# Sigmoid attention and a squared-ReLU FFN on one core: attn @ v in 64 x 64 quarters of the array, with an accumulator for each pair of heads

## The chip, the core and the metric

The kernel runs on one core of a Trainium2 chip, in one launch. The metric is the device time of that core in microseconds (us). Three executions of the kernel before gave 1017.53, 1017.70 and 1017.81 us; their median is 1017.7.

## What is computed

Eight batches of 12 heads, 448 positions and 64 dimensions a head, then a feed-forward network over 3584 tokens; all of it is float32.

```python
def _attn_ref(q, k, v):
    scale = 1.0 / np.sqrt(q.shape[-1])
    scores = scale * np.matmul(q, k.transpose(0, 1, 3, 2)) - np.log(S)
    attn = 1.0 / (1.0 + np.exp(-scores))
    return np.matmul(attn, v)

def _moe_ref(x, w_in, w_out, s, b):
    r = np.maximum(x @ w_in, 0.0)
    return (s * (r * r) + b) @ w_out
```

There is no softmax: each score goes through a sigmoid by itself, so that a block of keys can be finished alone. The change touches the attention only.

## The kernel before

The work has three stages that follow each other on TensorE: the attention (up to 251 us of the span), the FFN on the first 512 tokens, done plainly (to about 380 us), and the FFN on the other 3072 tokens, whose products are formed from sums of weight and token blocks (to the end). While TensorE does the attention, VectorE (DVE) and ScalarE (ACT) also convert the FFN's weights and form sums of weight rows; which step does how many of these jobs is set by the list `PIECES` and by `sums_out`, and `ticks(n, ...)` puts them into the engines' queues.

The attention takes 24 steps, one for each batch and each four heads ("quad"). Four heads are two pairs; `i` counts the pairs and `j` the two heads of a pair. The 448 keys of a head are three full blocks of 128 (`c` = 0, 1, 2) and a last block of 64. The last blocks of the two pairs share one tile.

One step does this, in this order on TensorE:

- `scores` (L658): keys times queries for six (pair, block) places, in the rounded high and low parts of the float32 numbers, three products each (`PARTS`), two heads at once in the two row halves of the array (64 x 128). Each place is a PSUM tile of two banks, a head in each. ACT makes the sigmoid of each (L638) into a tile `a` in SBUF.
- `attn_v` (L692): for each pair and each block, `v` (128 keys x 64 dimensions) times `a` (128 keys x 448 queries) in plain float32. A matmul fills the array's 128 rows and half of its columns, so the two heads of a pair run at once (128 x 64). A float32 matmul of the program is two matmul instructions in the trace. All of it accumulates in one PSUM tile `pav` of two banks: a bank for each pair, 64 partitions for each head.
- `scores_last` (L679): the scores of the last blocks of the *next* step, in 64 x 64 quarters, all four heads at once; ACT makes the sigmoid `a_l`.
- `attn_v_last` (L701): the last blocks of *this* step, also in quarters, added to `pav`, with the `a_l` that the step before made.

PSUM's eight banks are four tiles of two: three rotate as `psc` (scores and last scores), and the fourth is `pav`, which one score place, pair 0 with block 2, uses before `attn_v` does.

ACT's queue in a step: six sigmoids; the rounding of the next step's q and k (`qkh`, L621); the step's conversions (`wf`, L446) and roundings of weight sums (`t`, L491); the sigmoid `a_l`. DVE's queue: conversions and sums for the step; `parts_lo`, the low parts of the next step's q and k (`qkl`, L421), which needs `qkh`; the copy of `pav` to SBUF (`store_x`, L708), after which SyncE (SP) sends it to DRAM. Every engine takes its instructions in the order written, and a wait stops all that stand behind it in that queue.

Of the kernel before, what the change touches and what calls it, by code (L numbers as in the profile page):

```python
# [11 lines left out]
F32 = mybir.dt.float32  # L12
# [7 lines left out]
PSUM = bass.MemoryType.PSUM  # L20
# [308 lines left out]
def sigmoid_attention_relu2_ffn(  # L329
# [10 lines left out]
    nc = tc.nc  # L340
    B, NQ, P, _, _, S = qk.shape
    D = v.shape[5]
    NF, _, DM = w_in.shape
# [14 lines left out]
    def pool(stack, name, bufs, side=None, space=None):  # L358
        kw = dict(side=side) if side else {}
        if space is not None:  # L360
            kw["space"] = space
        return stack.enter_context(
            tc.tile_pool(name=name, bufs=bufs, reuse_waits="tile", **kw)
        )
# [41 lines left out]
    x_dram = [dram.tile([P, NCC, S], F32, name=f"xd_{b}") for b in range(B)]  # L406
# [10 lines left out]
    def add(o, x, y):  # L417
        nc.vector.tensor_tensor(o, x, y, op=ALU.add)  # L418
# [5 lines left out]
    order = [f + h * NP for f in range(NP) for h in range(2)]  # L424
# [159 lines left out]
    xo = pool(at, "xo", 2)  # L584
    ldv = pool(at, "ldv", 2)
    qkx = ExitStack()
    ld = pool(qkx, "ld", 2)
    hl = pool(qkx, "hl", 1)
    ps_qk = pool(qkx, "ps_qk", 3, space=PSUM)
    ps_av = pool(at, "ps_av", 1, space=PSUM, side="right")  # L590

    half = (slice(0, D), slice(D, P))
    quads = [(b, t) for b in range(B) for t in range(NQ)]
    NL = len(quads)

    def load(b, t, first=False):
        x = ld.tile([P, 2, 2, S], F32, tag="qk", name=f"qk_{b}_{t}")
        if first:
            nc.sync.dma_start(x[:, 0, 1, :P], qk[b, t][:, 0, 1, :P])
            nc.scalar.dma_start(x[:, 0, 0], qk[b, t][:, 0, 0])  # L600
            nc.sync.dma_start(x[:, 0, 1, P:], qk[b, t][:, 0, 1, P:])
            nc.scalar.dma_start(x[:, 1, 0], qk[b, t][:, 1, 0])
            nc.sync.dma_start(x[:, 1, 1], qk[b, t][:, 1, 1])
        else:
            nc.sync.dma_start(x, qk[b, t])
        return [x]

    def load_v(b, t, ld_):
        vt = ldv.tile([P, 7, 2, D], F32, tag="v", name=f"v_{b}_{t}")
        nc.sync.dma_start(vt, v[b, t])  # L610
        ld_.append(vt)
# [6 lines left out]
    def parts_hi(b, t, ld_):  # L618

        hi, lo = (hl.tile([P, 2, NX], F32R, tag=h, name=f"qk{h}_{b}_{t}") for h in "hl")  # L620
        nc.scalar.copy(hi, flat(ld_[0]))  # L621
        ld_.append((hi, lo))

    def parts_lo(ld_):
        hi, lo = ld_[-1]
        sub(lo, flat(ld_[0]), f32(hi))

    def parts_dve(b, t, ld_, pieces):
        hi, lo = (hl.tile([P, 2, NX], F32R, tag=h, name=f"qk{h}_{b}_{t}") for h in "hl")
        x = flat(ld_[0])  # L630
        for i, cols in pieces:
            nc.vector.tensor_copy(hi[:, i, cols], x[:, i, cols])
            sub(lo[:, i, cols], x[:, i, cols], f32(hi[:, i, cols]))
        ld_.append((hi, lo))

    def sigmoid(psc, name):
        a = ap_.tile([P, 2, S], F32, tag="a", name=f"a_{name}")
        nc.scalar.activation(a, psc[:, :, :S], AF.Sigmoid, bias=nls, scale=SCALE)  # L638
        return a

    def scores(b, t, ld_):
        x = ld_[0]
        two = ld_.pop() if len(ld_) > 2 else None
        whole = two is None or (b, t) == quads[0]
        a = {}
        psc = {}
        order = [(i, c) for i in range(2) for c in range(3)]
        if not whole:
            order[2:4] = order[3], order[2]
        for i, c in order:  # L650

            pl, tag = (ps_av, "pav") if (i, c) == (0, 2) else (ps_qk, "psc")
            o = psc[i, c] = pl.tile([P, 2, 512], F32, tag=tag, name=f"psc_{b}_{t}_{i}_{c}")
            if two and (i or c == 2 or not whole):
                cols = slice(S + c * P, S + (c + 1) * P)
                for m, (wi, xi) in enumerate(PARTS):
                    for j, r in enumerate(half):
                        nc.tensor.matmul(  # L658
                            o[:, j, :S], two[wi][r, i, cols], two[xi][r, i, :S],
                            start=m == 0, stop=m == 2,  # L660
                        )
            else:
                for j, r in enumerate(half):
                    nc.tensor.matmul(  # L664
                        o[:, j, :S], x[r, i, 1, c * P : (c + 1) * P], x[r, i, 0, :],
                        start=True, stop=True,
                    )
            if not whole and (i, c) == (1, 0):
                continue
            for k in [(i, c)] + [(1, 0)] * (not whole and (i, c) == (0, 2)):  # L670
                a[k] = sigmoid(psc[k], f"{b}_{t}_{k[0]}_{k[1]}")
        return a

    def scores_last(b, t, ld_):
        x = ld_[0]
        psc = ps_qk.tile([P, 2, 512], F32, tag="psc", name=f"psc_{b}_{t}_l")
        for j, r in enumerate(half):
            for i in range(2):
                nc.tensor.matmul(  # L679
                    psc[half[i], j, :S], x[r, i, 1, 3 * P :], x[r, i, 0, :],  # L680
                    start=True, stop=True,
                )
        return sigmoid(psc, f"{b}_{t}_l")

    def attn_v(b, t, ld_, a, between=None):
        pav = ps_av.tile([P, 2, 512], F32, tag="pav", name=f"pav_{b}_{t}")
        for i in range(2):
            if i and between:
                between()
            for c in range(3):  # L690
                for j, r in enumerate(half):
                    nc.tensor.matmul(  # L692
                        pav[r, i, :S], ld_[1][:, 3 * i + c, j, :], a[i, c][:, j, :],
                        start=c == 0, stop=False,
                    )
        return pav

    def attn_v_last(ld_, a, pav):
        for i in range(2):
            for j, r in enumerate(half):  # L700
                nc.tensor.matmul(  # L701
                    pav[r, i, :S], ld_[1][half[i], 6, j, :], a[half[i], j, :],
                    start=False, stop=True,
                )

    def store_x(b, t, pav):
        o = xo.tile([P, 2, S], F32, tag="xo", name=f"xo_{b}_{t}")
        nc.vector.tensor_copy(o, pav[:, :, :S])  # L708
        nc.sync.dma_start(x_dram[b][:, 2 * t : 2 * t + 2], o)

    loaded = {0: load(*quads[0], first=True)}
    load_v(*quads[0], loaded[0])
# [1 line left out]
    nc.scalar.activation(e_bias, nls, AF.Sigmoid)  # L714
    nc.vector.memset(e_bias, -896.0 * 2.0**23)

    idle = ps_qk.tile([P, 2, 512], F32, tag="psc", name="idle")
    ones = nc.const_aps.tensor(1.0, [P, 512], BF16)
    for _ in range(WARM):
        nc.tensor.matmul(idle[:, 0, :S], ones[:, :P], ones[:, :S], start=True, stop=True)  # L720
# [11 lines left out]
    def ticks(n, part):  # L732
        for _, _, fn in sorted(plan.pop((n, part), ()), key=lambda x: x[:2]):
            fn()
# [114 lines left out]
    for n, (b, t) in enumerate(quads):  # L849
        if n:  # L850
            ticks(n, "DVE")
        a = scores(b, t, loaded[n])
        between = None
        if n == 0:
            parts_dve(*quads[1], loaded[1], [(i, slice(NX)) for i in range(2)])
            ticks(0, "DVE")
            firsts = []

            def between():
                firsts.append(scores_last(*quads[0], loaded[0]))  # L860
                ticks(0, "ACT")

        else:
            if n + 1 in TWO:
                parts_hi(*quads[n + 1], loaded[n + 1])
            ticks(n, "ACT")
        if n + 2 < NL:
            loaded[n + 2] = load(*quads[n + 2])
        ticks(n, "SP")
        for fn in stores:  # L870
            fn()
        stores.clear()
        if n == NL - 1:
            qkx.close()
            ps_h = pool(blk_ps, "ps_h", 2, space=PSUM)
        pav = attn_v(b, t, loaded[n], a, between)
        last = al if n else firsts[0]
        if n + 1 < NL:
            al = scores_last(*quads[n + 1], loaded[n + 1])
        attn_v_last(loaded[n], last, pav)  # L880
        if n and n + 1 in TWO:
            parts_lo(loaded[n + 1])
        ticks(n, "END")
        store_x(b, t, pav)
        if n + 2 < NL:
            load_v(*quads[n + 2], loaded[n + 2])
    ph0 = ffn1(order[0], w1[0])
# [364 lines left out]
    for a, *_ in PRODUCTS_1:  # L1252
        seen = [a]
        while seen:
            x = seen.pop(0)
# [178 lines left out]
    o = plan1.op("SP", 0.0, readers, opened, late=OPEN_DUE)  # L1434
# [3 lines left out]
    x = None  # L1438
    for k in range(AHEAD):
        _, l, row, p = stream[k]  # L1440
        after = [o, x] + [row_op.get((l, row, f)) for f in (2 * p, 2 * p + 1)]
        x = plan1.op("SP", 1.28, after, lambda at: fetch(), late=OPEN_DUE + 6.0 + 2.8 * k)
# [84 lines left out]
```

## Time and profile before

| | before |
|---|---|
| median of three executions | 1017.7 us |
| the profiled execution: its own time | 1018.07 us |
| the profiled execution: its span | 1016.3 us |
| outside the span | 1.8 us |
| TensorE busy in the span | 1012.1 us |
| DVE busy in the span | 879.7 us |
| ACT busy in the span | 717.0 us |
| granted clock of TensorE | 1.00 |

The trace's times are in us from the span's start. A row of the timeline gives the start, the duration, the engine, the line, the operation, the tile written and the tiles read, the shape, and how many instructions in a row were merged; the square bracket behind it is the time for which the engine stood idle before them and whose end released it. Matmuls overlap: a row's duration runs to the end of its last instruction, so the next row starts before it. In the chain of waits each row is the stretch of the path that ended last. A group row gives the count of instructions, their busy time, the mean duration of one in ns, and the idle time before them.

### The profile page before, as it was taken

Reading aid. Unit: us, or ns where it says so; the run is one execution under the profiler, and the core shown is the slowest. Engines: PE = TensorE matmul, PEld = TensorE weight load, DVE = VectorE, ACT = ScalarE, POOL = GpSimd, SP = SyncE. Lnnn points to the kernel's source line nnn. Section 1 sums busy time; section 2 is a strip of 40 time slices with the busy share of each in tenths; the row PEclk is TensorE's granted clock in tenths of the full one; section 3 lists DMA queues with packets and bytes.
Section 4 is the critical chain, followed back from the end, with each engine's and each line's share of the span. In section 5 each row is a group of like instructions: output and inputs, shape, how many; then the busy total and the mean of one; then the engine's idle time right before and its main releaser. Section 6 shows DMA issues by size and latency. Waiting matters only on the chain.

```text
span 1016.3 us, 13837 instructions
## 1 busy us (share of the span) xinstructions
PE 1012.1 (100%) x5194; PEld 762.7 (75%) x5194; DVE 879.7 (87%) x989; ACT 717.0 (71%) x772; POOL 0.2 (0%) x4
## 2 busy tenths in 40 slices
PE   9999999999999999999999999999999999999998
PEld 4545455555888888888888888888888888888887
DVE  5899999898999958999978999996668668899995
ACT  7889999899777757747999944424544979964430
POOL 0000000000000000000000000000000000000000
PEclk9999999999999999999999999999999999999999
DMA  9788999896999999998966666799676666666784
GB/s 338 261 306 303 327 338 390 316 359 245 347 408 348 336 395 382 354 346 280 302 193 201 189 192 200 238 364 309 209 213 198 190 193 198 190 192 199 209 248 164
DMA packets 101073, 278.77 MB, mean 274 GB/s; under 512 B 10000, under 2 KB 23184, under 8 KB 101008
## 3 DMA queue, kind: packets, MB, share of 16 engines
q1 hardware_dynamic: 100720, 277.45, 79.9%
q8 instruction: 41, 0.67, 0.3%
q10 hardware_dynamic: 288, 0.46, 0.1%
q14 instruction: 24, 0.20, 0.1%
HBM read 193.99 MB, written 83.89 MB: 273 GB/s over the span
## 4 chain that ended last, share of the span: by engine, by line
PE 99%; ACT 1%; issue 0%; DVE 0%; ACTq 0%
PE b L1009 31%; PE b L1018 31%; PE pav L692 11%; PE psc L658 9%; PE ph L818 6%; PE po L1271 6%; PE psc_l L679 2%; PE pav L701 2%; ACT a L638 0%; PE idle L720 0%; PE psc L664 0%; PE o L1032 0%; ACT wf L446 0%; ACT qkh L621 0%; ACT t L491 0%
## 5 line engine op out<-in xcount | busy, mean ns | idle before, releaser
L1009 PE MATMUL b<-o_0h,wu 128*128 128x512 f32 x928 | 286.0, 389 | 0.0
L1009 PEld LDWEIGHTS b<-o_0h,wu 128*128 128x128 f32 x928 | 174.2, 188 | 36.2
L1009 PE MATMUL b<-o_0l,wu 128*128 128x512 f32 x464 | 180.5, 389 | 0.0
L1018 PE MATMUL b<-o_0h,wu 128*128 128x512 f32 x464 | 152.3, 389 | 0.0
L1018 PE MATMUL b<-o_1h,wu 128*128 128x512 f32 x456 | 149.6, 389 | 0.0
L638 ACT ACTIVATE a<-psc,nls 128x896 f32<-128x896 f32 x144 | 132.8, 1009 | 13.3 <-PE psc L658 10.6
L692 PE MATMUL pav<-a,v 128*64 128x448 f32 x576 | 113.8, 543 | 0.0
L418 DVE TENSOR_TENSOR r<-r,b 128x1024 f32<-128x1024 f32 x74 | 89.6, 1217 | 25.8 <-PE b L1009 22.9
L1009 PEld LDWEIGHTS b<-o_0l,wu 128*128 128x128 f32 x464 | 87.1, 188 | 18.0
L1018 PEld LDWEIGHTS b<-o_0h,wu 128*128 128x128 f32 x464 | 87.1, 188 | 18.0
L1018 PEld LDWEIGHTS b<-o_1h,wu 128*128 128x128 f32 x456 | 85.7, 188 | 17.7
L421 DVE TENSOR_TENSOR r<-r,b 128x1024 f32<-128x1024 f32 x66 | 80.0, 1216 | 20.4 <-PE b L1018 11.7
L1018 PE MATMUL b<-o_0l,wu 128*128 128x512 f32 x232 | 90.2, 389 | 0.0
L1018 PE MATMUL b<-o_1l,wu 128*128 128x512 f32 x228 | 88.7, 389 | 0.0
L692 PEld LDWEIGHTS pav<-a,v 128*64 128x64 f32 x576 | 39.1, 137 | 63.9 <-issue 45.1
L1064 ACT ACTIVATE r<-b 128x1024 f32<-128x1024 f32 x46 | 46.3, 1026 | 31.9 <-DVE r L418 13.4
L1271 PE MATMUL po<-g,w 128*128 128x512 f32 x288 | 67.7, 389 | 0.0
L959 ACT CAST o_0h<-r 128x1024 fp32r<-128x1024 f32 x26 | 27.3, 1051 | 57.2 <-DVE r L421 35.3
L1271 PEld LDWEIGHTS po<-g,w 128*128 128x128 f32 x288 | 54.1, 188 | 11.2
L491 ACT CAST t<-t 128x768 fp32r<-128x768 f32 (+2 forms) x62 | 44.1, 730 | 25.7 <-DVE t L421 15.7
L818 PE MATMUL ph<-x0h,w 128*128 128x512 f32 x192 | 61.7, 390 | 0.0
L1138 ACT ACTIVATE r<-r,b_sb,s_sb 128x1024 f32<-128x1024 f32 x48 | 59.5, 1241 | 1.0
(115 smaller groups left out, 1693.9 us busy)
## 6 DMA issues: line engine op xcount, KB each, us to landing
wu<-wd SPq DMA_DIRECT2D x232, 512.0 KB, 4.3
wd<-t SPq DMA_DIRECT2D x36, 768.0 KB, 6.8
qk<-qk_t SPq DMA_DIRECT2D x23, 896.0 KB, 7.0
st<-w_out SPq DMA_DIRECT2D x16, 768.0 KB, 8.7
st<-w_in SPq DMA_DIRECT2D x16, 768.0 KB, 9.0
wd<-t SPq DMA_DIRECT2D x22, 512.0 KB, 5.0
v<-v_t SPq DMA_DIRECT2D x24, 448.0 KB, 5.5
xd<-xo SPq DMA_DIRECT2D x24, 448.0 KB, 3.6
```

Source lines behind the costliest of these rows:

```text
L418: nc.vector.tensor_tensor(o, x, y, op=ALU.add)
L421: nc.vector.tensor_tensor(o, x, y, op=ALU.subtract)
L491: nc.scalar.copy(ts[g][:, :n, 0], f32(ts[g][:, :n, 1]))
L638: nc.scalar.activation(a, psc[:, :, :S], AF.Sigmoid, bias=nls, scale=SCALE)
L658: nc.tensor.matmul(o[:, j, :S], two[wi][r, i, cols], two[xi][r, i, :S], start=m == 0, stop=m == 2,)
L692: nc.tensor.matmul(pav[r, i, :S], ld_[1][:, 3 * i + c, j, :], a[i, c][:, j, :], start=c == 0, stop=False,)
L818: nc.tensor.matmul(ph, w[:, k, wi, kc * P : (kc + 1) * P], x0[h][xi][:, cc, :], start=m == 0, stop=m == 3 * NCC - 1,)
L1009: nc.tensor.matmul(bk[:, j], wt[:, j, wi, c * P : (c + 1) * P], tiles[xi][:, c, :], start=first and m == 0, stop=m == 3 * KC - 1, skip_gro ...
L1018: nc.tensor.matmul(bk[:, e], wt[:, f, wi, e * P : (e + 1) * P], tiles[gi][:, f], start=first and f == 0 and m == 0, stop=p == np_ - 1 and ...
L1064: nc.scalar.activation(v.t, bank_t[b], AF.Copy, scale=-1.0)
L1138: nc.scalar.activation(v.t, v.t, AF.Identity, bias=b_sb, scale=s_sb)
L1271: nc.tensor.matmul(pos[e], w[:, k, wi, kc * P : (kc + 1) * P], g[:, gi, :], start=first and i == 0, stop=last and i == 2,)
```

## The change

`attn_v` splits each block of 128 keys into two halves of 64 (`m`, `rows`), so that its matmuls are 64 x 64 quarters, four at once: two key halves times two heads. The two key halves of a pair go to different banks of a PSUM tile that the pair has for itself: `pav` becomes a list of two tiles, and the sum of a pair's two banks is its result. There are twice as many matmuls, each on half as many rows.

For pair `i` the bank `1 - i` is complete when `attn_v` of that pair is done, and is copied out at once into half of an SBUF tile `x`: by DVE for pair 0, in the middle of `attn_v`, and by ACT for pair 1, at its end. `attn_v_last` adds the last block to bank `i`, and then `store_x` has DVE add bank `i` to the half of `x`, once for each pair, in place of one copy of both.

The four two-bank places of PSUM are now named 0 to 3 (`place`); 2 and 3 are those of `pav`. The six score places of a step take the places `turn`, 2, 3 and `turn` again; for every step but the first, pair 1's block 0 stands before pair 0's block 2, and so takes place 3. `scores_last` takes the first of `turn`, which is then reversed.

```diff
-    ps_qk = pool(qkx, "ps_qk", 3, space=PSUM)
+    ps_qk = pool(qkx, "ps_qk", 1, space=PSUM)
     ps_av = pool(at, "ps_av", 1, space=PSUM, side="right")
+    turn = [0, 1]
+    def place(k, name):
+        pl = ps_qk if k < 2 else ps_av
+        return pl.tile([P, 2, 512], F32, tag=f"s{k}", name=name)
...
-        for i, c in order:
-            pl, tag = (ps_av, "pav") if (i, c) == (0, 2) else (ps_qk, "psc")
-            o = psc[i, c] = pl.tile([P, 2, 512], F32, tag=tag, name=f"psc_{b}_{t}_{i}_{c}")
+        places = turn + [2, 3] + turn
+        if not whole:
+            places[2:4] = 3, 2
+        for k, (i, c) in zip(places, order):
+            o = psc[i, c] = place(k, f"psc_{b}_{t}_{i}_{c}")
...
     def attn_v(b, t, ld_, a, between=None):
-        pav = ps_av.tile([P, 2, 512], F32, tag="pav", name=f"pav_{b}_{t}")
+        pav = []
+        x = xo.tile([P, 2, S], F32, tag="xo", name=f"xo_{b}_{t}")
         for i in range(2):
             if i and between:
                 between()
+            o = place(2 + i, f"pav_{b}_{t}_{i}")
+            pav.append(o)
             for c in range(3):
-                for j, r in enumerate(half):
-                    nc.tensor.matmul(
-                        pav[r, i, :S], ld_[1][:, 3 * i + c, j, :], a[i, c][:, j, :],
-                        start=c == 0, stop=False,
-                    )
-        return pav
+                for m, rows in enumerate(half):
+                    for j, r in enumerate(half):
+                        nc.tensor.matmul(
+                            o[r, m, :S], ld_[1][rows, 3 * i + c, j, :], a[i, c][rows, j, :],
+                            start=c == 0, stop=c == 2 and m != i,
+                        )
+            (nc.scalar.copy if i else nc.vector.tensor_copy)(x[:, i], o[:, 1 - i, :S])
+        return pav, x
     def attn_v_last(ld_, a, pav):
         for i in range(2):
             for j, r in enumerate(half):
                 nc.tensor.matmul(
-                    pav[r, i, :S], ld_[1][half[i], 6, j, :], a[half[i], j, :],
+                    pav[i][r, i, :S], ld_[1][half[i], 6, j, :], a[half[i], j, :],
                     start=False, stop=True,
                 )
-    def store_x(b, t, pav):
-        o = xo.tile([P, 2, S], F32, tag="xo", name=f"xo_{b}_{t}")
-        nc.vector.tensor_copy(o, pav[:, :, :S])
-        nc.sync.dma_start(x_dram[b][:, 2 * t : 2 * t + 2], o)
+    def store_x(b, t, pav, x):
+        for i in range(2):
+            add(x[:, i], x[:, i], pav[i][:, i, :S])
+        nc.sync.dma_start(x_dram[b][:, 2 * t : 2 * t + 2], x)
...
-            al = scores_last(*quads[n + 1], loaded[n + 1])
+            al = scores_last(*quads[n + 1], loaded[n + 1], turn[n == 0])
+            if n:
+                turn.reverse()
```

On TensorE, at the end of step 1 before the change (the names give batch, quad, pair and block; `a_1_l` is the sigmoid of the last blocks, `v` the values; a bracket names the engines or transfers whose semaphores the instruction waits for):

```order
L692 MATMUL pav_1_352<-a_1_1_1_333,v_1_173 64x448 [waits Activation_49]
L692 MATMUL pav_1_352<-a_1_1_1_333,v_1_173 64x448
L692 MATMUL pav_1_352<-a_1_1_2_342,v_1_173 64x448 [waits Activation_49]
L692 MATMUL pav_1_352<-a_1_1_2_342,v_1_173 64x448
L679 MATMUL psc_2_l<-qk_2_241 64x448 [waits DMAHW4_49]
L679 MATMUL psc_2_l<-qk_2_241 64x448 x3
L701 MATMUL pav_1_352<-a_1_l,v_1_173 64x448 x4
```

The same place after the change, on TensorE:

```order
L703 MATMUL pav_1_1_383<-a_1_1_1_349,v_1_173 64x448 [waits Activation_49]
L703 MATMUL pav_1_1_383<-a_1_1_1_349,v_1_173 64x448 x3
L703 MATMUL pav_1_1_383<-a_1_1_2_358,v_1_173 64x448 [waits Activation_49]
L703 MATMUL pav_1_1_383<-a_1_1_2_358,v_1_173 64x448 x3
L686 MATMUL psc_2_l<-qk_2_241 64x448 [waits DMAHW4_49,PE_49]
L686 MATMUL psc_2_l<-qk_2_241 64x448 x3
L713 MATMUL pav_1_0_369<-a_1_l,v_1_173 64x448 [waits DVE_49]
L713 MATMUL pav_1_0_369<-a_1_l,v_1_173 64x448
L713 MATMUL pav_1_1_383<-a_1_l,v_1_173 64x448 [waits Activation_49]
L713 MATMUL pav_1_1_383<-a_1_l,v_1_173 64x448
```

Each pair and block has four matmuls where it had two, and the last blocks' four matmuls, which waited for nothing, now wait for DVE (the first two) and for ACT (the other two).

On ACT, in the same step before the change, from the last score sigmoid to the next step's first one:

```order
L638 ACTIVATE a_1_1_2_342<-psc_1_1_2_335,nls 128x896 [waits PE_49,Activation_49]
L621 CAST qkh_2_344<-qk_2_241 128x1664 [waits DMAHW4_49]
L446 ACTIVATE wf_8_99<-wf_8_99,e_bias 128x768 [waits DVE_49]
L638 ACTIVATE a_2_l<-psc_2_l,nls 128x896 [waits PE_49,Activation_49]
L638 ACTIVATE a_2_0_0_396<-psc_2_0_0_389,nls 128x896 [waits PE_49,Activation_49]
```

And after the change, on ACT:

```order
L644 ACTIVATE a_1_1_2_358<-psc_1_1_2_351,nls 128x896 [waits PE_49,Activation_49]
L627 CAST qkh_2_360<-qk_2_241 128x1664 [waits DMAHW4_49]
L446 ACTIVATE wf_8_99<-wf_8_99,e_bias 128x768 [waits DVE_49]
L707 COPY xo_1_368<-pav_1_1_383 128x448 [waits PE_49]
L644 ACTIVATE a_2_l<-psc_2_l,nls 128x896 [waits PE_49,Activation_49]
L644 ACTIVATE a_2_0_0_428<-psc_2_0_0_421,nls 128x896 [waits PE_49,Activation_49]
```

The copy of pair 1's finished bank stands behind the rounding and the conversions of its step, and ahead of `a_l`.

On DVE, around the end of step 1, after the change; before it, two rows stood between the same neighbours, the subtraction `qkl` and one copy of 896 elements a partition (L708):

```order
L442 TENSOR_SCALAR wf_8_99<-st_8_243 128x768 [waits DMAHW5_49]
L707 COPY xo_1_368<-pav_1_0_369 128x448 [waits PE_49]
L421 TENSOR_TENSOR qkl_2_361<-qk_2_241,qkh_2_360 128x1664 [waits DMAHW4_49,Activation_49]
L418 TENSOR_TENSOR xo_1_368<-xo_1_368,pav_1_0_369 128x448 [waits DVE_49,PE_49]
L418 TENSOR_TENSOR xo_1_368<-xo_1_368,pav_1_1_383 128x448 [waits PE_49,Activation_49]
L455 SCALAR_TENSOR_TENSOR st_4_171<-st_4_171 128x768
```

The first copy stands ahead of `qkl`, and the two additions stand where the one copy stood.

More of the change, by code (lines that the diff above doesn't have):

```diff
@@ L672, in scores, with scores_last @@
         return a
-    def scores_last(b, t, ld_):
+    def scores_last(b, t, ld_, k):
         x = ld_[0]
-        psc = ps_qk.tile([P, 2, 512], F32, tag="psc", name=f"psc_{b}_{t}_l")
+        psc = place(k, f"psc_{b}_{t}_l")
         for j, r in enumerate(half):
@@ L715, in sigmoid_attention_relu2_ffn @@
     nc.vector.memset(e_bias, -896.0 * 2.0**23)
-    idle = ps_qk.tile([P, 2, 512], F32, tag="psc", name="idle")
+    idle = place(1, "idle")
     ones = nc.const_aps.tensor(1.0, [P, 512], BF16)
@@ L859, in between @@
             def between():
-                firsts.append(scores_last(*quads[0], loaded[0]))
+                firsts.append(scores_last(*quads[0], loaded[0], 0))
                 ticks(0, "ACT")
@@ L875, in sigmoid_attention_relu2_ffn @@
             ps_h = pool(blk_ps, "ps_h", 2, space=PSUM)
-        pav = attn_v(b, t, loaded[n], a, between)
+        pav, x = attn_v(b, t, loaded[n], a, between)
         last = al if n else firsts[0]
         if n + 1 < NL:
-            al = scores_last(*quads[n + 1], loaded[n + 1])
+            al = scores_last(*quads[n + 1], loaded[n + 1], turn[n == 0])
+            if n:
+                turn.reverse()
         attn_v_last(loaded[n], last, pav)
@@ L883, in sigmoid_attention_relu2_ffn @@
         ticks(n, "END")
-        store_x(b, t, pav)
+        store_x(b, t, pav, x)
         if n + 2 < NL:
```

## The prediction, made before the changed kernel was run

> **What bounds the kernel now.** I read the page first, then the chain of waits, then the timeline of TensorE, ACT and DVE in steps of the attention. The page's busy shares and its chain:
>
> ```profile
> PE 1012.1 (100%) x5194; PEld 762.7 (75%) x5194; DVE 879.7 (87%) x989; ACT 717.0 (71%) x772; POOL 0.2 (0%) x4
> PE 99%; ACT 1%; issue 0%; DVE 0%; ACTq 0%
> ```
>
> TensorE is the whole path: whatever makes it stand still, or lets it work less, shows in the time. The chain of waits in order of time gives the starts of steps 2, 3 and 23 (the six places of the scores, L658), and the last blocks' scores of step 3:
>
> ```profile
> 26.89 3.84 PE psc L658 x36
> ...
> 37.08 3.84 PE psc L658 x36
> ...
> 45.61 0.91 PE psc_l L679 x8
> ...
> 241.88 3.84 PE psc L658 x36
> ```
>
> A step takes 37.08 - 26.89 = 10.19 us where nothing is late. Over 21 steps it is (241.88 - 26.89) / 21 = 10.24, so about 1.0 us of waiting lies in all of them. The timeline of TensorE at the end of step 1; the first row is from a wider window:
>
> ```profile
> 20.50 4.73 PE L692 MATMUL pav<-a,v 128*64 128x448 f32 x24
> ...
> 24.68 0.55 PE L692 MATMUL pav<-a,v 128*64 128x448 f32 x2
> 25.16 0.98 PE L679 MATMUL psc_l<-qk 64*64 64x448 f32 x8
> 25.96 0.93 PE L701 MATMUL pav<-a_l,v 64*64 64x448 f32 x8
> 26.82 0.47 PE L658 MATMUL psc<-qkh 64*128 64x448 f32 x2
> ```
>
> The 24 instructions of `attn_v` run in 12 rounds of two. The last round starts at 24.68, so eleven took 4.18 us, 0.38 each. In quarters four run at once: eight instructions are two rounds, and L679's two took 25.96 - 25.16 = 0.80.
>
> **What the quarters save.** `attn_v` will have 48 instructions, four at a time, which is again 12 rounds of 0.38 us: splitting the keys saves no array time. What goes is the change of shape from 128 x 64 to 64 x 64. The last round of `attn_v` kept the array for 25.16 - 24.68 = 0.48 instead of 0.38, and L679's two rounds took 0.80 instead of 0.76: 0.14 us together. There are 26 such places (one a step, two more in step 0, where the last blocks of step 0 stand inside `attn_v`): **-3.6 us**. The changes between scores and `attn_v`, and back, remain.
>
> **What the early copy costs.** In the changed order the last blocks' matmuls (L713) wait, for pair 1, for ACT's copy of the finished bank. Behind them on TensorE stands the whole next step. The copy can't start before `attn_v` ends, and it stands behind all other ACT work of the step. What covers it is `scores_last`, 0.76 us. ACT at the end of step 0 and of step 1:
>
> ```profile
> 16.02 1.01 ACT L638 ACTIVATE a_l<-psc_l,nls 128x896 f32<-128x896 f32 x1 [0.32 <-PE psc_l L679]
> ...
> 23.00 1.60 ACT L621 CAST qkh<-qk 128x1664 fp32r<-128x1664 f32 x1
> 24.47 0.96 ACT L446 ACTIVATE wf<-wf,e_bias 128x768 int32<-128x768 int32 x1
> 26.27 1.01 ACT L638 ACTIVATE a_l<-psc_l,nls 128x896 f32<-128x896 f32 x1 [0.83 <-PE psc_l L679]
> ```
>
> Copies by ACT out of PSUM, 512 and 1024 columns, in the groups up to 390 us:
>
> ```profile
> L1062 ACT COPY r<-b 128x1024 f32<-128x1024 f32 x2 | 2.0, 1006 | 0.1
> L1484 ACT COPY o<-po 128x512 f32<-128x512 f32 x3 | 1.8, 609 | 0.0
> ```
>
> That is 0.78 ns a column, so 448 columns take 609 - 50 = 0.56 us. Step 1 is a light one: `scores_last` would start at 24.68 + 0.38 = 25.06, and the last blocks would want to start at 25.82. ACT's conversion ends at 25.43; the next instruction starts about 0.1 before such an end (24.47 against 23.00 + 1.60 = 24.60), so the copy runs from 25.36 (its data are there 0.13 after the end of `attn_v`, as `a_l` came 0.13 after 25.16 + 0.98) to 25.92, and TensorE goes on 0.07 later, at 25.99. The stall is **0.17 us**, which is already more than the saved 0.14. Heavier steps, 3 and 9: ACT's last jobs and its `a_l`, and for step 9 TensorE's `scores_last` and where TensorE waited for `a_l`, each from its own timeline:
>
> ```profile
> 44.86 1.78 ACT L446 ACTIVATE wf<-wf,e_bias 128x768 int32<-128x768 int32 x2
> 46.59 1.01 ACT L638 ACTIVATE a_l<-psc_l,nls 128x896 f32<-128x896 f32 x1
> ```
>
> ```profile
> 107.95 1.57 ACT L491 CAST t<-t 128x768 fp32r<-128x768 f32 x2
> 109.41 1.02 ACT L638 ACTIVATE a_l<-psc_l,nls 128x896 f32<-128x896 f32 x1
> ```
>
> ```profile
> 106.96 0.98 PE L679 MATMUL psc_l<-qk 64*64 64x448 f32 x8
> ...
> 110.48 0.47 PE L658 MATMUL psc<-qkh 64*128 64x448 f32 x2 [0.37 <-ACT a_l L638]
> ```
>
> In step 3 ACT is free at about 46.54. Step 3 is two steps behind step 1 (`scores_last` stands at 45.61 in the chain, and for step 1 `attn_v` ends at 24.68 + 0.55 = 25.23), so TensorE wants to go on at 46.20 and can at 46.54 + 0.56 + 0.07 = 47.17: 0.97. In step 9 the places are 107.62 and 110.05: 2.43. Before, such lateness fell on `a_l`, which nobody needs before the next step's third place; 2.4 us of it cost 0.37. Now TensorE stands behind it at once. Each job beyond the light step's one conversion so adds its whole time to the stall. These are ACT's jobs in steps 1 to 22:
>
> ```profile
> L446 ACT ACTIVATE wf<-wf,e_bias 128x768 int32<-128x768 int32 x28 | 25.8, 951 | 0.1
> L638 ACT ACTIVATE a_l<-psc_l,nls 128x896 f32<-128x896 f32 x22 | 22.2, 1009 | 7.4 <-PE psc_l L679 7.3
> L491 ACT CAST t<-t 128x768 fp32r<-128x768 f32 x10 | 8.1, 836 | 0.0
> L832 ACT CAST x0h<-x0l 128x1536 fp32r<-128x1536 f32 x1 | 1.5, 1503 | 0.0
> L547 ACT CAST w<-wf 128x768 fp32r<-128x768 f32 x1 | 0.9, 857 | 0.0
> L491 ACT CAST t<-t 128x256 fp32r<-128x256 f32 x1 | 0.4, 398 | 0.0
> ```
>
> 41 jobs, 36.7 us busy. Less one conversion of 0.95 in each of 22 steps (20.9) and the overlap of 0.11 for each of the 19 others (2.1) that is 13.7 us, and with 22 light stalls of 0.17 (3.7) **+17.4 us**. A stall doesn't heal by itself: every step's sigmoids start after its own first scores, so ACT's lateness is made anew in each step. Step 0 has `a_l` waiting 0.32 instead of 0.83, so 0.51 later: 0.17 + 0.51, say **+0.6**. In step 23 there are no further last scores, so nothing covers the copy; the ACT job ahead of it and TensorE there:
>
> ```profile
> 251.39 0.83 ACT L547 CAST w<-wf 128x768 fp32r<-128x768 f32 x1
> ```
>
> ```profile
> 245.68 4.73 PE L692 MATMUL pav<-a,v 128*64 128x448 f32 x24
> 250.34 0.98 PE L701 MATMUL pav<-a_l,v 64*64 64x448 f32 x8
> ```
>
> TensorE would go on at 250.24, and can at 252.12 + 0.56 + 0.07 = 252.75: **+2.5**. As TensorE now waits ahead of `a_l`, the 1.0 us that it waited before goes: **-1.0**.
>
> **DVE.** Its copy of 896 columns becomes a copy and two additions of 448. The rows nearest, the last two for 1024 and 512 columns:
>
> ```profile
> L708 DVE COPY xo<-pav 128x896 f32<-128x896 f32 x24 | 26.2, 1092 | 11.6 <-PE pav L701 11.6
> ```
>
> ```profile
> L418 DVE TENSOR_TENSOR r<-r,b 128x1024 f32<-128x1024 f32 x74 | 89.6, 1217 | 25.8 <-PE b L1009 22.9
> ```
>
> ```profile
> L421 DVE TENSOR_TENSOR g<-r,g 128x512 fp32r<-128x512 f32 x16 | 11.1, 691 | 15.8 <-ACT g L1343 15.4
> ```
>
> At 1.03 ns a column 448 take 0.63 us, 0.55 from one to the next. The second addition ends 0.07 + 0.55 + 0.63 = 1.25 us after the step's end, where the place of pair 1, block 0 (the third, two times 0.61 us and a change of shape later) is wanted at about 1.25 too; with the hand-over 0.04 a step, **+0.9**. The first copy waits for the middle of `attn_v`, and `qkl` and the rest of DVE's queue stand behind it. Its cover is the time in which DVE waits for ACT's cast. Step 11, one of the tightest:
>
> ```profile
> 126.85 0.56 DVE L442 TENSOR_SCALAR wf<-st 128x768 int32<-128x768 int32 x1
> 127.50 1.89 DVE L421 TENSOR_TENSOR qkl<-qk,qkh 128x1664 fp32r<-128x1664 f32 x1
> 129.83 1.09 DVE L708 COPY xo<-pav 128x896 f32<-128x896 f32 x1 [0.43 <-PE pav L701]
> ```
>
> The copy puts `qkl` off by about 0.5 us, and 0.43 is left behind it: it ends at the step's end, just in time. I take **+1.0** for all steps; the bounds are 0 (the stalls give DVE time) and 0.4 (the half microsecond with little to hide it) in each of nine light steps, by the wait of `a_l` for its scores, which is left only there:
>
> ```profile
> ACT a_l L638 <- PE psc_l L679: 7.3, 10, 0.8
> ```
>
> 7.3 us in steps 1 to 22, 0.8 at most, are some nine light steps.
>
> **The sum.** -3.6 + 17.4 + 0.6 + 2.5 - 1.0 + 0.9 + 1.0 = +17.8 us. The profiled execution's own 1018.07 becomes 1035.9. That one stands 0.4 above the median of the runs, so the median becomes 1017.7 + 17.8 = **1035.5**. Copy time not shown at this size: by the nearest ACT rows it lies between 0.40 (256 columns, the cast above) and 0.61 (512), which over 24 steps is -3.8 to +1.2; I take the slope between two copies out of PSUM.
>
> A page speaks against the wait itself. The Trainium skill, "PSUM — Partial Sum Buffer", Summary, says that PSUM may be read while a matmul runs if the read targets another bank. The early copy reads the bank that the last blocks don't write, so by that page the two could overlap. No trace of before shows such an overlap in one tile. The order after has the wait all the same, so the sum goes by the order.
>
> **Rivals.**
> - *The copy's wait is met early* (0.07): the order names engines, not counts; if ACT's semaphore at L713 stands for `a_l`, made a step before, nothing waits for the copy. Then -3.6 - 1.0 + 0.9 + 1.0 remain: **1015.0**, faster. Against it: pair 0's matmul, which reads the same `a_l`, waits for DVE alone. It decides if all stalls stay under 4 us, which needs ACT idle at the end of `attn_v` in nearly every step; ACT is busy past it in some 13 of 22 steps. The rule above gives the same 1015.0, if this wait were not there.
> - *DVE becomes the bound* (0.08): it gains 0.63 + 1.10 - 1.01 = 0.7 us a step, and the copy parts its work into two waits. If the nine light steps pay 0.6 each rather than the 1.0 in all: 1035.5 + 4.4 = **1039.9**.
> - *TensorE can't issue quarters fast enough* (0.05): the scores run 36 matmuls and 36 weight loads in 3.84 us, 53 ns each; a steady stream of quarters needs 96 in 4.56, 48 ns. At 53, `attn_v` takes 0.5 us longer in each of 24 steps, +12, of which the copy, then less late in the 13 heavy steps, gives back about 6.5: **1041**.
> - *They cancel* (0.02): the stalls only outweigh the saved switches.
>
> **The numbers.** The forecast has 0.78. The range takes in the copy's lower bound with DVE's terms at nothing (1035.5 - 3.8 - 1.9 = 1029.8) and a little more for ACT lateness that shrinks, and above both slower rivals: 1027 to 1043. 0.2% is 2 us, about what a measurement of this kernel can tell. Faster 0.07, same 0.02, slower 0.78 + 0.08 + 0.05 = 0.91.
>
> **What would show it.** TensorE idle before L713 with ACT's xo copy (L707) as releaser, about 0.2 us in light steps and 1 to 2.5 in heavy ones, some 20 us in all; rounds of `attn_v` still 0.38; no gap of 0.1 before L686; a light step of about 10.25. Rounds under 0.36, or no idle time before L713, would make it wrong.

## The result, and the profile after

The changed kernel takes 1033.92 us (median of six runs, 1033.49 to 1035.12); the kernel before, on the same chip, 1017.65 (six runs, 1017.52 to 1017.86). The ratio is 1.0162, with a 95% interval of 1.0149 to 1.0176: slower by 16.3 us. The profiled execution took 1034.05 us, its span is 1032.2, and the granted clock is 1.00 as before.

The page's busy times and the chain's shares by engine:

```profile
PE 1023.0 (99%) x5770; PEld 770.3 (75%) x5770; DVE 894.7 (87%) x1037; ACT 726.7 (70%) x796; POOL 0.2 (0%) x4
PE 91%; ACT 5%; DMA 1%; issue 1%; DVE 1%; SPq 0%; ACTq 0%; DVEq 0%
```

ACT now holds 5% of the path, where it held 1%. The chain of waits in order of time shows where. Steps 2, 3 and 4 start at 27.36, 37.58 and 48.60; then comes step 9, from its first sigmoid to the next step's scores:

```profile
27.36 3.90 PE psc L665 x36
...
37.58 3.87 PE psc L665 x36
...
48.60 3.91 PE psc L665 x36
...
102.82 0.57 ACT a L644
...
109.72 1.78 ACT wf L446 x2
111.50 1.45 ACT t L491 x2
112.95 0.44 ACT xo L707
113.44 0.97 PE pav L713 x4
114.41 3.84 PE psc L665 x36
```

Step 2 is a light one and takes 37.58 - 27.36 = 10.22 us, about as before (10.19). Step 3 has one conversion more on ACT and takes 48.60 - 37.58 = 11.02. In step 9, which has four jobs, the path leaves TensorE from the first sigmoid to the copy and runs through ACT's sigmoids, cast, jobs and copy: the step takes 12.5 us, where before it took 10.2.

The waits of the attention, of the engines that stand for one another (engine, tile and line; releaser; us in total, times, longest):

```profile
ACT a L644 <- PE psc L665: 21.0, 23, 1.3
...
PEld pav L713 <- ACT xo L707: 16.5, 15, 2.2
...
PE pav L713 <- ACT xo L707: 5.0, 7, 1.5
```

The weight loads for the last blocks (PEld) stand 16.5 us behind ACT's copy, in 15 steps. The row of PE shows such waits a second time, on the matmuls: in step 9 the weight loads stand from 111.20 and the matmuls from 111.98, both to 113.44, so the two rows can't be added. And ACT stands for TensorE in each of 23 steps, 21.0 us in all, for the first scores of the next step. Before the change it stood there too, but half as long, and TensorE's matmuls stood for the sigmoid of the last scores in one step only:

```profile
ACT a L638 <- PE psc L658: 10.6, 19, 0.9
...
PE psc L658 <- ACT a_l L638: 0.4, 1, 0.4
```

Now the two wait for one another in step after step.

The quarters did as was said. TensorE at the end of step 1:

```profile
24.04 1.68 PE L703 MATMUL pav<-a,v 64*64 64x448 f32 x16
25.55 0.93 PE L686 MATMUL psc_l<-qk 64*64 64x448 f32 x8
26.30 1.07 PE L713 MATMUL pav<-a_l,v 64*64 64x448 f32 x8
27.29 0.47 PE L665 MATMUL psc<-qkh 64*128 64x448 f32 x2
```

16 instructions are four rounds: 25.55 - 24.04 = 1.51, 0.38 each, the last one no longer than the others (0.48 before); L686's two rounds take 0.75 (0.80 before). That is 0.15 us a place. The wait behind them is what is new: 27.29 - 26.30 = 0.99 from L713 to the scores, where it was 26.82 - 25.96 = 0.86.

Over the span, the attention ends at 267.24 instead of 251.25, 16.0 later; what follows takes as long as before. Of these, 0.5 fall in step 0, 13.9 in steps 1 to 22, and 1.6 in step 23.

### The profile page after: what moved, and what is told of

It is laid out like the page before. It is cut to its first block, busy times and chain, and to the rows that moved or that the text cites. A ratio compares the mean times of both kernels' runs of the same rounds, so it can differ in the third digit from the quotient of the medians.

```text
span 1032.2 us, 15126 instructions
## 1 busy us (share of the span) xinstructions
PE 1023.0 (99%) x5770; PEld 770.3 (75%) x5770; DVE 894.7 (87%) x1037; ACT 726.7 (70%) x796; POOL 0.2 (0%) x4
## 4 chain that ended last, share of the span: by engine, by line
PE 91%; ACT 5%; DMA 1%; issue 1%; DVE 1%; SPq 0%; ACTq 0%; DVEq 0%
PE b L1023 31%; PE b L1032 30%; PE pav L703 7%; PE psc L665 7%; PE ph L830 6%; PE po L1285 6%; PE pav L713 3%; ACT a L644 2%; PE psc_l L686 1%; ACT wf L446 1%; DMA qk<-qk_t 1%; ACT t L491 1%; ACT qkh L627 1%; DMA v<-v_t 0%; ACT xo L707 0%
## 5 line engine op out<-in xcount | busy, mean ns | idle before, releaser
L703 PE MATMUL pav<-a,v 64*64 64x448 f32 x1152 | 114.0, 540 | 0.0
L421 DVE TENSOR_TENSOR r<-r,b 128x1024 f32<-128x1024 f32 x66 | 80.0, 1216 | 20.4 <-PE b L1032 11.7
L703 PEld LDWEIGHTS pav<-a,v 64*64 64x64 f32 x1152 | 41.7, 133 | 61.3 <-issue 43.3
L1078 ACT ACTIVATE r<-b 128x1024 f32<-128x1024 f32 x46 | 46.3, 1026 | 31.3 <-DVE r L418 13.1
```

The costliest lines, as they stand in the source:

```text
L421: nc.vector.tensor_tensor(o, x, y, op=ALU.subtract)
L703: nc.tensor.matmul(o[r, m, :S], ld_[1][rows, 3 * i + c, j, :], a[i, c][rows, j, :], start=c == 0, stop=c == 2 and m != i,)
L1078: nc.scalar.activation(v.t, bank_t[b], AF.Copy, scale=-1.0)
```

## The experiments

Four theories were set against each other. W: TensorE stands at L713 behind ACT's copy. L: ACT's load costs, wherever the copy stands. Q: the quarters are dearer. D: DVE's extra work costs. The kernel before took 1017.82 to 1017.88 on the chips of these runs.

### Taking the copies away

The first kernel is the changed one without ACT's copy; pair 1 is stored from one bank, so that the other bank's half of the keys is left out of its result:

```diff
-            (nc.scalar.copy if i else nc.vector.tensor_copy)(x[:, i], o[:, 1 - i, :S])
+            if i == 0:
+                nc.vector.tensor_copy(x[:, i], o[:, 1 - i, :S])
...
-        for i in range(2):
-            add(x[:, i], x[:, i], pav[i][:, i, :S])
+        add(x[:, 0], x[:, 0], pav[0][:, 0, :S])
+        nc.vector.tensor_copy(x[:, 1], pav[1][:, 1, :S])
```

> The changed kernel without ACT's early copy: pair 1 is stored from its second bank alone, so the sum of its first three blocks' first accumulator is left out; DVE still has three instructions of 448 columns a step. Theory W (TensorE stands at the last blocks' matmuls behind ACT's copy, which stands behind ACT's other jobs): that wait goes, and 1016 to 1018 us is left. Rival L (the added work on ACT and DVE costs its time wherever it stands): about half of the 16 us stays, 1026. Rival Q (quarters run slower than halves of the array): no change, 1034.

It took 1018.76 us, 1.0009 times before (0.9999 to 1.0018). The whole loss hangs on this one copy, and Q falls. But nothing is gained either, though the saved changes of shape are worth some 3.6 us. Part of where they went is in its waits (`a_l` is the sigmoid of the last scores):

```profile
PEld psc L665 <- ACT a_l L644: 4.5, 6, 1.5
```

In heavy steps the scores wait for `a_l`, whose place is now taken second by the next step, where it was taken third before; W had not counted this, and was 0.8 too low. Light steps take 10.13 us: 0.15 less for the shapes, and 0.09 more at the third place.

Without DVE's early copy, and with ACT's kept:

```diff
-            (nc.scalar.copy if i else nc.vector.tensor_copy)(x[:, i], o[:, 1 - i, :S])
+            if i:
+                nc.scalar.copy(x[:, i], o[:, 1 - i, :S])
...
-        for i in range(2):
-            add(x[:, i], x[:, i], pav[i][:, i, :S])
+        nc.vector.tensor_copy(x[:, 0], pav[0][:, 0, :S])
+        add(x[:, 1], x[:, 1], pav[1][:, 1, :S])
```

> The changed kernel without DVE's early copy of pair 0; pair 0 is stored from one bank by one copy, pair 1 as in the changed kernel (left out: one bank's half of the keys of pair 0). W: DVE isn't waited for at L713, so the time stays at 1032 to 1035, and the waits on ACT's copy at L713 stay as they were (18 to 20 us). D (DVE's extra 0.7 us a step is the greater part of the cost): 1020 to 1027.

One run took 1033.7 us, and the wait at the last blocks (L714 in this kernel) is the same row but for 0.1:

```profile
PEld pav L714 <- ACT xo L708: 16.6, 15, 2.2
```

By this one run D falls: DVE's early copy costs nothing that shows. Without either copy:

```diff
-            (nc.scalar.copy if i else nc.vector.tensor_copy)(x[:, i], o[:, 1 - i, :S])
...
-            add(x[:, i], x[:, i], pav[i][:, i, :S])
+            nc.vector.tensor_copy(x[:, i], pav[i][:, i, :S])
```

> The changed kernel without either early copy: each pair is stored from one bank with two copies of 448 columns by DVE (left out: the other bank's half of the keys in each pair). W: nobody waits at L713 and ACT has before's load, so the quarters stand alone: 24 steps x 0.15 us of saved shape changes (3.6) against the third score place, which still waits for DVE's second operation (about 0.09 a step, 2.2), and the place of the last scores, which is wanted second instead of third (2 us in heavy steps): 1016.5 to 1018.5, no measurable change. As without ACT's copy alone (1018.8), or up to 2 lower if DVE's early copy costs something. Q (quarters dearer): 1022 or more.

1018.93 us (1.0002 to 1.0020 times before), a little above W's range and level with the first kernel. So the quarters alone, with nothing to be summed, are worth nothing here.

### The load without the wait, and the wait twice

The kernel before, with a copy of 448 columns from SBUF to SBUF at the same place of ACT's queue. No instruction of TensorE waits for it, and it waits for none of TensorE's, so both sides of the hand-over are gone:

```diff
+        x = xo.tile([P, 2, S], F32, tag="xo", name=f"xo_{b}_{t}")
+        nc.scalar.copy(x[:, 1], a[1, 2][:, 1])
...
-        store_x(b, t, pav)
+        store_x(b, t, pav, x)
```

> The kernel before with one ACT copy of 448 columns a step added, SBUF to SBUF, at the place in ACT's queue where the change has it; no matmul waits for it, and the output stays the same. Theory W: the copy only makes the last blocks' sigmoid later in the heavy steps, 1 to 3 us in all: 1018.5 to 1020.5. Rival L: half of the loss or more, 1025 to 1033. Rival Q: 1017.7.

1019.11 us, 1.0012 times before (1.0002 to 1.0021): 1.3 us. ACT's 0.5 us a step cost little as load; L falls in its plain form. The changed kernel with ACT's copy made twice:

```diff
             (nc.scalar.copy if i else nc.vector.tensor_copy)(x[:, i], o[:, 1 - i, :S])
+            if i:
+                nc.scalar.copy(x[:, i], o[:, 1 - i, :S])
```

> The changed kernel with ACT's early copy made twice, one behind the other. Theory W: every step, light or heavy, stands still longer by the second copy's time, 0.45 to 0.63 us, so 24 of them give 1045 to 1049. Rival L: the light steps hide it, since ACT has time there: 1038 to 1041. Rival Q: 1034 to 1035.

One run took 1053.67 us, 19.7 more than the changed kernel. ACT at the end of step 1, and TensorE's waits (L715 is the last blocks' line here):

```profile
25.96 0.53 ACT L707 COPY xo<-pav 128x448 f32<-128x448 f32 x1
26.52 0.53 ACT L709 COPY xo<-pav 128x448 f32<-128x448 f32 x1
```

```profile
PEld pav L715 <- ACT xo L709: 28.8, 24, 2.8
```

The second copy puts 0.56 us more ahead of the wait, and light steps take about 10.7 to 10.8 instead of 10.2: 24 times 0.55 are 13.2, which is W's account. The other 6.5 us W had not foreseen; the last section has what may be behind them. A copy that costs 0.05 a step as load costs 0.55 when TensorE waits for it.

### What the wait hangs on

The next kernel makes each of the accumulators' four banks a PSUM tile of its own, so that the matmuls into one bank don't wait for the copy out of the other. Scores that use these places then need two sigmoids of 448 columns:

```diff
-        return pl.tile([P, 2, 512], F32, tag=f"s{k}", name=name)
...
+        return [ps_av.tile([P, 512], F32, tag=f"s{k}{j}", name=f"{name}{'ab'[j]}") for j in range(2)]
...
+            for j in range(2):
+                nc.scalar.activation(a[:, j], psc[j][:, :S], AF.Sigmoid, bias=nls, scale=SCALE)
...
-                    pav[i][r, i, :S], ld_[1][half[i], 6, j, :], a[half[i], j, :],
+                    pav[i][i][r, :S], ld_[1][half[i], 6, j, :], a[half[i], j, :],
```

> The changed kernel with each of the four banks of the two pav places as a PSUM tile of its own, so that the matmul into one bank no longer waits for the copy out of the other; all work is kept, and the two score places made of such tiles take two sigmoids of 448 columns in place of one of 896 (about 0.2 us more on ACT a step). Theory W: no idle time before the last blocks' matmuls; ACT's lateness falls on the last blocks' sigmoid again, some 4 to 8 us in all: 1020 to 1024. Rival L: ACT has more to do, so 1035 to 1040. Rival Q: 1034.

1027.45 us, 1.0098 times before (1.0081 to 1.0114): better than the change by 6.5, and worse than W said. ACT and then TensorE at the end of step 3:

```profile
46.35 0.56 ACT L713 COPY xo<-pav_1a 128x448 f32<-128x448 f32 x1
46.76 1.06 ACT L647 ACTIVATE a_l<-psc_l,nls 128x896 f32<-128x896 f32 x1
```

```profile
45.88 0.54 PE L719 MATMUL pav_1b<-a_l,v 64*64 64x448 f32 x2
...
46.25 0.54 PE L719 MATMUL pav_1b<-a_l,v 64*64 64x448 f32 x2
...
47.87 0.47 PE L671 MATMUL psc<-qkh 64*128 64x448 f32 x2 [0.26 <-ACT a_l L647]
```

The copy reads bank 1a from 46.35 to 46.91 while matmuls write bank 1b from 46.25 to 46.79, and the last blocks start without a stall: the wait at L713 came from the two banks being one tile. By this the Trainium skill, "PSUM — Partial Sum Buffer", Summary, that PSUM can be read under a running matmul in another bank, agrees with the trace. But the place of `a_l` is wanted right afterwards, and `a_l` stands behind the copy: TensorE's wait moved there, in 13 steps. Two split sigmoids also keep ACT 1.04 us where one whole one keeps it 0.90: 0.28 for the two places of a step, where W had taken 0.2.

The next edit, on the changed kernel, moves ACT's conversions of a step behind the copy and `a_l`:

```diff
-            ticks(n, "ACT")
...
+        if n:
+            ticks(n, "ACT")
         attn_v_last(loaded[n], last, pav)
```

> The changed kernel with ACT's conversions and roundings of the step moved behind the copy and the sigmoid of the last scores, all work kept. W (TensorE stands behind ACT's copy, and the copy behind ACT's jobs): the copy now comes straight after the cast of q and k, so TensorE waits at L713 about 0.1 to 0.15 us in every step, heavy or light (2 to 3 us in all, 18 to 20 before). ACT's lateness is not gone: it falls on the first score sigmoids of the next step, and TensorE waits there or at the first of attn @ v; a part of what is won at L713 comes back as that wait. W expects 1026 to 1031. L (ACT's load alone is what costs, wherever it stands): as the changed kernel, 1033 to 1035. Q (the quarters themselves are dearer): also 1033 to 1035, with no wait on ACT moved.

1033.65 us, 1.0157 times before (1.0140 to 1.0174): nothing is won, and W's 1026 to 1031 is wrong. The time is the one that L and Q gave, but Q had no wait moved, and L has the run with the load alone against it. The wait at L713 is gone as W said, and a wait on the score sigmoids has taken its place, of the same size. Its waits, and ACT in step 9:

```profile
ACT xo L707 <- PE pav L703: 17.6, 23, 2.2
...
PEld psc L665 <- ACT a L644: 16.3, 26, 2.0
...
PEld pav L713 <- ACT xo L707: 1.5, 2, 0.8
```

```profile
102.27 5.50 ACT L644 ACTIVATE a<-psc,nls 128x896 f32<-128x896 f32 x6
107.62 1.61 ACT L627 CAST qkh<-qk 128x1664 fp32r<-128x1664 f32 x1
109.93 0.53 ACT L707 COPY xo<-pav 128x448 f32<-128x448 f32 x1 [0.70 <-PE pav L703]
110.68 1.01 ACT L644 ACTIVATE a_l<-psc_l,nls 128x896 f32<-128x896 f32 x1 [0.22 <-PE psc_l L686]
111.59 1.75 ACT L446 ACTIVATE wf<-wf,e_bias 128x768 int32<-128x768 int32 x2
113.24 1.55 ACT L491 CAST t<-t 128x768 fp32r<-128x768 f32 x2
114.70 3.69 ACT L644 ACTIVATE a<-psc,nls 128x896 f32<-128x896 f32 x4
```

This gave a better form of W, and one that explains why L's number came: what costs is a closed loop. In the changed kernel ACT's timeline of the same step reads:

```profile
108.25 1.59 ACT L627 CAST qkh<-qk 128x1664 fp32r<-128x1664 f32 x1
109.72 1.78 ACT L446 ACTIVATE wf<-wf,e_bias 128x768 int32<-128x768 int32 x2
...
112.84 0.54 ACT L707 COPY xo<-pav 128x448 f32<-128x448 f32 x1
...
115.31 2.84 ACT L644 ACTIVATE a<-psc,nls 128x896 f32<-128x896 f32 x3 [1.02 <-PE psc L665]
```

The first sigmoid of step 9 starts at 102.82, that of step 10 at 115.31: 5.43 for six sigmoids, 1.47 for the cast, 3.12 for four jobs, 0.60 to the last blocks' start (113.44), and 1.87 for TensorE's last blocks and first scores, for which ACT stands 1.02. Without the jobs the loop is 9.37 us. With the light step's one job (0.84) it is 10.21, which is what a light step takes; with step 3's two (1.66) 11.03, and step 3 takes 11.02. The second copy's 0.56 makes the light loop 10.77, and light steps took 10.7 to 10.8 with the copy made twice. With the conversions behind the copy, ACT stands ahead of the copy and of `a_l` instead (0.70 and 0.22); from 102.27 to 114.70 are 12.43, less 3.11 for the jobs 9.32. Both orders give the same step, since in both ACT stands about 1 us a step for TensorE, and TensorE for ACT. In the kernel before, ACT stood for TensorE in the light steps, but its lateness hardly reached TensorE: in step 9 its six sigmoids, cast, jobs and `a_l` ran on into step 10, which is lighter, and were caught up there. The chain of waits of before has the starts of steps 9 and 11:

```profile
98.50 0.82 PE psc L658 x6
...
119.57 3.85 PE psc L658 x36
```

The two steps took 21.07 us, only 0.69 more than two light ones.

So ACT must not stand. The next kernel has the bank tiles and ACT's copy behind `a_l`. It also takes pair 0's accumulator third and pair 1's fourth for the scores, and makes the sigmoids in the order of the scores. (The expectation calls this before's order of blocks; but TensorE takes the blocks in the same order before, after and here, and before's sigmoids had pair 0's block 2 ahead of pair 1's block 0.)

```diff
-        if not whole:
-            places[2:4] = 3, 2
...
-            for k in [(i, c)] + [(1, 0)] * (not whole and (i, c) == (0, 2)):
-                a[k] = sigmoid(psc[k], f"{b}_{t}_{k[0]}_{k[1]}")
+            a[i, c] = sigmoid(o, f"{b}_{t}_{i}_{c}")
...
-            (nc.scalar.copy if i else nc.vector.tensor_copy)(x[:, i], o[1 - i][:, :S])
+            if i == 0:
+                nc.vector.tensor_copy(x[:, i], o[1 - i][:, :S])
...
             al = scores_last(*quads[n + 1], loaded[n + 1], turn[n == 0])
...
+        nc.scalar.copy(x[:, 1], pav[1][0][:, :S])
```

> The changed kernel with each bank of the two accumulators a tile of its own (as in the run with bank tiles, 1027.45), the copy of pair 1 by ACT placed behind the last scores' sigmoid in ACT's queue, and the score places in before's order of blocks. All work kept. W: no instruction of TensorE stands behind the copy any more except the fourth score place, which wants the bank free 1.8 us into the next step; the last scores' sigmoid is as late as in before, but is wanted at the second place instead of the third, and ACT has 0.55 us for the copy and 0.25 us for the split sigmoids more in each step. W expects 1019 to 1024: below the bank tiles alone, not below before. L (load): 1027 as with the bank tiles, since the load is the same.

1022.21 us, 1.0040 times before (1.0025 to 1.0055). That is 11.7 of the 16 us back, all work kept. Against the bank tiles alone it is 5.2 us better; three things changed between the two, and no run tells their shares apart. ACT at the end of step 9 has no bracket of idle time any more, from the last scores' sigmoid over the copy to the next step's sigmoids:

```profile
109.48 1.06 ACT L647 ACTIVATE a_l<-psc_l,nls 128x896 f32<-128x896 f32 x1
110.39 0.58 ACT L896 COPY xo<-pav_1a 128x448 f32<-128x448 f32 x1
110.80 1.98 ACT L647 ACTIVATE a<-psc,nls 128x896 f32<-128x896 f32 x2
```

What remains is mostly `a_l` at the second place, for which TensorE's matmuls wait 2.6 us in four steps and its weight loads 5.7 in ten. The obvious next edit takes that place third again:

```diff
+        if not whole:
+            order = [order[i] for i in (0, 2, 1, 3, 4, 5)]
+            places = [turn[0], 2, turn[1], 3, turn[0], turn[1]]
```

> As the run with bank tiles and ACT's copy behind the last scores' sigmoid (1022.21), and the place of the last scores is taken third by the next step's scores, as before the change, instead of second (pair 0's tile of attn @ v is taken second). All work kept. W: in that run TensorE waited 1.2 us at the second place in step 9, and some 8 us in all, for the last scores' sigmoid; the third place is wanted 0.6 us later, so each of the 14 waits shrinks by up to 0.6, about 6 us of 8, less what DVE's later qkl and the pair's addition take back: 1018 to 1021, level with before or a little above, not under it by more than 0.2%. L (load of ACT, wherever it stands): 1022 as it was.

1034.78 us, 1.0165 times before (1.0148 to 1.0182): wrong by 14. The sixth place now reuses the tile of the third, where it reused that of the second; the third's sigmoid comes later in ACT's queue, behind the two split ones, and TensorE waits for it in every step (light steps take 10.95):

```profile
PEld psc L672 <- ACT a L647: 19.8, 23, 1.1
```

The last kernel goes the other way: two-bank tiles, no copy by ACT, and DVE copies pair 1's bank at the end and adds the other. Its places and sigmoids are changed as in the kernel that took 1022.21:

```diff
+            if i == 0:
+                nc.vector.tensor_copy(x[:, i], o[:, 1 - i, :S])
...
+        add(x[:, 0], x[:, 0], pav[0][:, 0, :S])
+        nc.vector.tensor_copy(x[:, 1], pav[1][:, 0, :S])
+        add(x[:, 1], x[:, 1], pav[1][:, 1, :S])
```

> The changed kernel (two-bank tiles) with no copy by ACT: DVE copies pair 1's first bank after the last blocks and then adds the second, and the score places are in before's order of blocks. All work kept. W: nobody on TensorE waits at L713 for ACT, so the 21 us of waits there go; ACT has before's load. In their place DVE has three operations of 0.55 us from one to the next after the end of a step, and TensorE's fourth score place waits for the last of them: 0.07 + 1.1 + 0.63 = 1.8 us after the end, wanted at about 1.9; where DVE is busy past the end, TensorE waits. W expects 1020 to 1028. L (an extra 0.55 us of copying on either engine costs as much as in the changed kernel): 1033.

1025.54 us, 1.0083 times before (1.0066 to 1.0099), inside W's range. No instruction of TensorE waits for a copy by ACT any more. Light steps take 10.25 to 10.28, where they took 10.13 without ACT's copy, and TensorE's weight loads wait 6.4 us in 17 places for DVE's late `qkl`: the price of DVE's third operation, as far as the changed places have no part in it, which no run shows. No form of the change that was tried beats the kernel before; the best whole one is 4.4 us above it.

## Why the prediction was right, and where its terms were off

The direction, the mechanism and the size were right: 1035.5 was said, 1033.9 came, inside 1027 to 1043. Step by step:

- *Shape changes, -3.6.* Right as a saving on TensorE: 0.15 a place was seen, 0.14 said, and the 12 rounds kept their length. But without the copies the gain does not show in the time at all (1018.8 and 1018.9). The prediction had no term for the place of `a_l`, which the next step now wants second; that costs nothing while TensorE waits for the copy anyway, and eats up the gain where it doesn't.
- *The stalls of steps 1 to 22, +17.4.* Right in kind. The part that the trace gives step by step fits: step 3 became 11.02 - 10.19 = 0.83 longer than before (0.97 less 0.14 saved, 0.83, was said), step 9 12.50 - 10.19 = 2.31 (2.43 - 0.14 = 2.29 said). Taken with the terms for the places, the waits that go, DVE and the changes of shape, steps 1 to 22 were to give 15.1 and gave 13.9. Of the 1.2 too much, 1.0 would be DVE's drift, below. The 0.37 that it gave for before's lateness in step 9 is the bracket of one row; by the starts of the steps it was 0.69, which its sum, made from step times, already holds.
- *Light steps, about 10.25.* They took 10.17 to 10.22, about as before (10.19): the stall of some 0.13 and the later third place eat up the saved 0.15.
- *Step 0, +0.6.* Less 0.4 for its three shape changes, 0.2 was said; 0.5 came. What the other 0.3 is stays open.
- *Step 23, +2.5.* Mis-sized: less 0.14, 2.4 was said; 1.6 came. The prediction took `w` (L547) to stand ahead of the copy, as in before's timeline. ACT after, at the end of step 23:

```profile
264.35 1.49 ACT L844 CAST x0h<-x0l 128x1536 fp32r<-128x1536 f32 x1
265.73 0.55 ACT L707 COPY xo<-pav 128x448 f32<-128x448 f32 x1
267.35 3.04 ACT L547 CAST w<-wf 128x768 fp32r<-128x768 f32 x4 [1.07 <-PE pav L713]
```

  This group of `w` now comes behind the copy and waits for the last blocks itself, so the copy ended about 0.7 sooner than was worked out. That the stall has nothing to cover it was right.
- *DVE's drift, +1.0, and its second addition, +0.9.* The drift does not show: without DVE's early copy the time is the same to 0.2 us, in one run. The second addition can't be told apart inside the stalls; where they are gone the third place costs 0.09 a step, twice the 0.04 said.
- *The rivals.* That the wait would be met early fell with the waits at L713; that DVE would be the bound, with the run without its copy; that quarters could not be issued fast enough, with rounds of 0.38.
- *"A stall doesn't heal by itself."* This sentence was the heart of it and holds, for a reason that was only half seen. The prediction charged the jobs because they stand ahead of the copy. By that count moving them behind it should have helped, as the expectation for that run said. It did not (1033.65): the loop through both engines has 9.3 to 9.4 us besides the jobs in either order. That the size came out right although the count was only half the reason is luck: both ways of counting add each further job's whole time to the step.

## What to carry to other kernels

A copy that one engine makes between two matmul groups costs little by its own length (1.3 us for 24 copies nobody waits for) and much by what it ties together: it closes a loop in which each step takes the sum of both engines' turns. ACT's 70% in the profile is the mean of the whole span; in steps 1 to 22 of the kernel before it was busy 207.6 of 225.2 us, 92%, and had little room for a wait. Before adding such a hand-over, add up the loop once round for the heaviest step, and look whether the engine could so far run late in one step and catch up in the next. Where the wait comes from a tile that is larger than what is read, cutting the tile takes the wait away, but look at once at which tile is wanted next.

## Hardware behaviour that was not expected

In the kernel with the copy made twice, TensorE's clock fell to half for stretches after some of its stalls. TensorE behind the 2.00 us stall at the end of step 9, then three of five windows of the trace with such a clock; it stands third from the right, ahead of the DMA share and GB/s (the last of the five lies in the FFN):

```profile
119.84 0.97 PE L715 MATMUL pav<-a_l,v 64*64 64x448 f32 x4 [2.00 <-ACT xo L709]
...
121.85 0.58 PE L665 MATMUL psc<-qkh,qkl 64*128 64x448 f32 x2
122.23 0.58 PE L665 MATMUL psc<-qkh 64*128 64x448 f32 x2
```

```profile
84.40:87.60 3.20, 3.20 (x20) 2.83 (x20) 3.10 (x5) 2.03 (x2) 0.00 (x0) 0.50 0.51 161
121.80:125.20 3.40, 3.40 (x22) 3.04 (x20) 3.30 (x5) 2.24 (x3) 0.00 (x0) 0.50 0.87 290
...
285.80:289.00 3.20, 3.20 (x9) 2.42 (x9) 3.12 (x5) 3.20 (x5) 0.00 (x0) 0.50 0.62 247
```

The scores' matmuls start 0.38 us apart instead of the 0.20 that they take elsewhere. Five such stretches of about 3.4 us, in which half the work is done, are up to 8.5 us, enough for the 6.5 that were left to explain; no second run of this kernel shows whether they are the cause.

The stalls ahead of them were 1.27, 2.00, 1.26, 1.17 and 1.30 us. The ten other stalls of these matmuls in the same execution were 0.99 us or less, and none was followed by such a clock. But the size alone does not decide: a stall of 1.46 in the changed kernel (behind its step 9) was followed by a clock of 1.00, and so was one of 1.73 with the bank tiles. Two of the six executions of the changed kernel show a mean clock of 0.998 and took 1035.05 and 1035.12 us, some 1.3 more than the other four; one such stretch would cost up to 1.7. No trace shows whether it was one. What tells the cases apart stays open.

The Trainium skill, "TensorE: Matmul & The Clock Gate", Part 1, has the gate watch windows of about 3.4 us that run free of the work. The length of the stretches agrees with that. The Trainium skill, "TensorE: Matmul & The Clock Gate", "Why this matters for your kernels", gives gaps of over about 3 us as the ones to avoid. Here stalls of 1.17 to 2.00 us were followed by the halved clock.
